# Block 0 of a fused layernorm, state-space and gated-MLP kernel: eps as the bias of the ScalarE root, and first gate matmuls in two halves of the contraction

## Chip, cores and metric

The kernel runs on one core of a Trainium2 chip. The metric is device time in microseconds of one execution of the whole program, smaller is better. Engines are named as in the profile: PE is TensorE, PEld its weight loads, DVE is VectorE, ACT is ScalarE, POOL is GpSimd, SP is the queue that issues most loads. A load "lands" when its data has arrived. A "hand-over" is the time from the end of one engine's instruction to the start of the instruction on another engine that waited for it. PSUM is the memory that TensorE writes its results to; the "contraction" is the sum over the 512 features, done in four chunks of 128.

## The reference

The input is one sequence of 2048 tokens of 512 features. Only the first part matters here: the layernorm feeds everything, and its first block of 512 tokens (four tiles of 128, "block 0") is what the machine waits for at the start.

```python
xn = (x - mean(x)) / sqrt(var(x) + 1e-5)          # x: [2048, 512], bf16
y_ssm = 2 * Re(scan(Lam_bar, xn @ B_bar.T) @ C.T) + xn * Dskip
y_mlp = (gelu(xn @ w_gate) * (xn @ w_up)) @ w_down  # w_gate, w_up: [512, 1376]
out = x + y_ssm + y_mlp
```

## The kernel before

The program lists operations with their reads and writes. A scheduler inside the kernel then orders them by a model of durations: TensorE and the SP queue keep the order in which the program lists them, while VectorE, ScalarE and GpSimd may be reordered.

The parts that the change touches, with cuts marked `# ...`:

```python
# loads: four x tiles on the SP queue, first gate weights on the ScalarE queue, then the rest on SP
for j in range(4):
    ld_x0(j)
ld_w(WG, WGc, ins["B_w_gate"], 0, "scalar").nb = 900.0     # gate columns 0..383
ld_w(WU, WUc, ins["B_w_up"], 0)                            # up columns 0..383
ld_w(WG, WGc, ins["B_w_gate"], 1)
ld_w(WU, WUc, ins["B_w_up"], 1)
# ...
def LN(b, js=range(4), on_act=False, after=()):
    # ...
    for j in js:
        V(bn_stats(X[tt]) -> ST[tt]);  V(bn_aggr(ST[tt]) -> MVt[b][j])      # abridged
    POOL(copy of the means)                                                  # abridged
    V(lambda e: e.tensor_scalar(sbq.ap, mv.ap[:, :, 1], EPS_BF16, None, ALU.add), D_TINY, [mv], [sbq], "sbq")
    if on_act:
        ACT(lambda e: e.activation(qb.ap, sbq.ap, ACTF.Sqrt), d_act(4), [sbq, SCR], [qb], "sqrt")
    else:
        POOL(...pow 0.5...)
    V(lambda e: e.reciprocal(rq.ap, qb.ap), 150, [qb], [rq], "rq")
    # ... VectorE: XN = (X - mean) * rq, tile by tile
# ...
def TR0(j, engs, first=None):        # TensorE transposes tile j; its copies out of PSUM go to engs
    per = KD // len(engs)            # "VA": VectorE copies contraction chunks 0,1; ScalarE chunks 2,3
    # ... for n, eng in enumerate(engs): transposes of half n, then the copy of half n
# ...
def GU_first(fts, early, banks):
    def mm(ft, u, j0, j1):           # u=0 gate, u=1 up; four matmuls over the contraction
        # ... for dk in range(KD): matmul(start=(dk == 0), stop=(dk == KD - 1)), reads XT0[j0:j1]
    for u in range(2):
        for ft in early:             # early = three groups of 128 columns
            mm(ft, u, 0, 1)          # 12 gate matmuls, then 12 up matmuls, on tile 0
    params()
    for ft in early:
        for u in range(2):
            mm(ft, u, 1, 2)          # then tile 1
    # ... then the first of the "late" groups (second weight chunks), transposes of tiles 2 and 3
# ...
PE(fwarm, ...)                       # 11 warm-up matmuls that do nothing useful
LN(0, [0, 1], True)                  # tiles 0 and 1: statistics, root on ScalarE
TR0(0, "VA")
TR0(1, "V", hbanks[0][4])
LN(0, [2, 3], True, [GATE["evT"]])   # tiles 2 and 3: a second root on ScalarE
```

Of the kernel before, what the change touches and what calls it, by code (L numbers as in the profile page):

```python
# [9 lines left out]
ALU = mybir.AluOpType  # L10
ACTF = mybir.ActivationFunctionType
# [335 lines left out]
NT, NB, KD, KP, KF = 16, 4, 4, 4, 11  # L347
# [4 lines left out]
EPS_BF16 = 1.0013580322265625e-05  # L352

def d_pe(n_list):
    return sum(n / 2.4 + 2.5 for n in n_list)
def d_dve_tt2x(n): return 100.0 + 0.52 * n
def d_dve_1x(n): return 100.0 + 1.04 * n
def d_dve_scan(n): return 90.0 + 2.08 * n
def d_dve_ts4x(n): return 220.0 + 0.26 * n
D_TINY = 160.0  # L360
def d_act(n, ptr=0): return 190.0 + 0.833 * n + 90.0 * ptr
# [3 lines left out]
def build(nc, ins, out):  # L365
    with ExitStack() as es:
# [6 lines left out]
        BANK = [Buf("bank%d" % i, "ps", i, i + 1) for i in range(8)]  # L373

        def ring(parent, name, n):
            return [A.sub(parent, "%s%d" % (name, i), i) for i in range(n)]
# [11 lines left out]
        XNT = ring(XNT_all, "XNT", NB)  # L388
# [22 lines left out]
        def cols(buf, b, j0, j1):  # L411
            per = (buf.hi - buf.lo) // (4 * NB)
            return Buf("%s_%d_%d" % (buf.name, b, j0), "sb", buf.lo + per * (4 * b + j0), buf.lo + per * (4 * b + j1),
                       buf.ap[:, b, j0:j1])
        XTk = [[Buf("XT%d_%d" % (b, i), "xt", 4 * b + i, 4 * b + i + 1) for i in range(4)] for b in range(NB)]
        XT0 = XTk[0]
        XTr = lambda b: XTk[b]
        WRM = A.alloc("WRM", [128], BF16)
        PROW = A.alloc("PROW", [128], BF16)
# [6 lines left out]
        EPS = A.alloc("EPS", [1], F32)  # L426
# [76 lines left out]
        wchunk = lambda ft: 0 if ft < 3 else (1 if ft < 7 else 2)  # L503

        V = lambda fn, dur, r, w, tag="", after=(): S.op("vector", fn, dur, r, w, tag, after)
        ACT = lambda fn, dur, r, w, tag="", after=(): S.op("scalar", fn, dur, r, w, tag, after)
        POOL = lambda fn, dur, r, w, tag="": S.op("gpsimd", fn, dur, r, w, tag)
        PE = lambda fn, dur, r, w, tag="": S.op("tensor", fn, dur, r, w, tag)
# [9 lines left out]
        SCR = A.alloc("SCR", [1], F32)  # L518
# [4 lines left out]
        def next_bank():  # L523
            b_ = rstate["n"] % 8
            rstate["n"] += 1
            return b_
# [69 lines left out]
        def LN(b, js=range(4), on_act=False, after=()):  # L596
            j0, j1 = js[0], js[-1] + 1
            mn, sbq, qb, rq = (cols(t, b, j0, j1) for t in (MN, SBQ, QB, RQ))
            mv = Buf("MV%d_%d" % (b, j0), "sb", MVt[b][j0].lo, MVt[b][j1 - 1].hi, MV[b].ap[:, j0:j1])
            for j in js:  # L600
                tt = 4 * b + j
                V(lambda e, tt=tt: e.bn_stats(ST[tt].ap, X[tt].ap), d_dve_1x(512), [X[tt]], [ST[tt]], "bnst", after)  # L602
                V(lambda e, tt=tt, j=j: e.bn_aggr(MVt[b][j].ap, ST[tt].ap), D_TINY, [ST[tt]], [MVt[b][j]], "bnag")  # L603
            POOL(lambda e: e.tensor_copy(mn.ap, mv.ap[:, :, 0]), 200, [mv], [mn], "mn")
            V(lambda e: e.tensor_scalar(sbq.ap, mv.ap[:, :, 1], EPS_BF16, None, ALU.add), D_TINY, [mv], [sbq], "sbq")  # L605
            if on_act:
                ACT(lambda e: e.activation(qb.ap, sbq.ap, ACTF.Sqrt), d_act(4), [sbq, SCR], [qb], "sqrt")  # L607
            else:
                POOL(lambda e: e.tensor_tensor(qb.ap, sbq.ap, HALF.ap[:, 0:j1 - j0], ALU.pow), 1100, [sbq, HALF], [qb], "pow")
            V(lambda e: e.reciprocal(rq.ap, qb.ap), 150, [qb], [rq], "rq")  # L610
            for j in js:
                tt = 4 * b + j
                xs = XN[tt % 8]
                V(lambda e, tt=tt, j=j, xs=xs: e.tensor_scalar(  # L614
                    xs.ap, X[tt].ap, mn.ap[:, j - j0:j - j0 + 1], rq.ap[:, j - j0:j - j0 + 1], ALU.subtract, ALU.mult),
                  d_dve_ts4x(512), [X[tt], mn, rq], [xs], "ln_n")
# [9 lines left out]
        def TR0(j, engs, first=None):  # L626
            if not TBANK:
                TBANK.extend([next_bank(), next_bank()])
            per = KD // len(engs)
            toks = [XT0[j]] if len(engs) == 1 else [Buf("XT0_%d_%d" % (j, n), "xt", j + n / len(engs), j + (n + 1) / len(engs))  # L630
                                                    for n in range(len(engs))]
            for n, eng in enumerate(engs):
                bank = TBANK[(j + n) % 2] if first is None else first
                pt = PS[bank].bitcast(BF16)

                def f(e, n=n, pt=pt):
                    ins_ = None
                    for q in range(per):
                        k = per * n + q
                        ins_ = e.transpose(pt[:, 128 * q:128 * (q + 1)], XN[j].ap[:, 128 * k:128 * (k + 1)], IDN.ap)  # L640
                    return ins_
                PE(f, 56.0 * per, [XN[j], IDN], [BANK[bank]], "T0")
                dst = XNT[0].ap[:, per * n:per * (n + 1), 128 * j:128 * (j + 1)]
                src = pt[:, 0:128 * per].rearrange("p (q t) -> p q t", q=per)
                if eng == "A":
                    GATE["evTA"] = ACT(lambda e, src=src, dst=dst: e.activation(dst, src, ACTF.Copy), d_act(128 * per),  # L646
                                       [BANK[bank]], [toks[n]], "evT")
                else:
                    GATE["evT"] = V(lambda e, src=src, dst=dst: e.tensor_copy(dst, src), 110 + 0.6 * 128 * per,
                                    [BANK[bank]], [toks[n]], "evT")  # L650
# [67 lines left out]

        def GU_first(fts, early, banks):

            def mm(ft, u, j0, j1):
                W, Wc = ((WG, WGc), (WU, WUc))[u]
                h, q0 = j0 // 2, 256 * u + 128 * (j0 % 2)
                bank = banks[h][ft]

                def f(e):
                    ins_ = None
                    for dk in range(KD):
                        ins_ = e.matmul(PS[bank][:, q0:q0 + 128 * (j1 - j0)], W.ap[:, dk, 128 * ft:128 * (ft + 1)],  # L729
                                        XNT[0].ap[:, dk, 128 * j0:128 * j1], start=(dk == 0), stop=(dk == KD - 1))  # L730
                    return ins_
                PE(f, d_pe([128 * (j1 - j0)] * 4), [Wc[wchunk(ft)]] + XT0[j0:j1], [BANK[bank]], "GU0")

            def evac(ft, h, after=()):
                bank, c0 = banks[h][ft], 256 * h
                GATE["nh"] = kk = (GATE["nh"] + 1) % 3
                GATE["last_gelu"] = ACT(lambda e: e.activation(GG[kk].ap[:, 0:256], PS[bank][:, 0:256], ACTF.Gelu_apprx_tanh),
                                        d_act(256), [BANK[bank]], [GG[kk]], "gelu", after)
                ACT(lambda e: e.activation(UPB[kk].ap[:, 0:256], PS[bank][:, 256:512], ACTF.Copy),
                    d_act(256), [BANK[bank]], [UPB[kk]], "evU")  # L740
                V(lambda e: e.tensor_tensor(HTt[0][ft].ap[:, c0:c0 + 256], GG[kk].ap[:, 0:256], UPB[kk].ap[:, 0:256], ALU.mult),
                  d_dve_tt2x(256), [GG[kk], UPB[kk]], [HTt[0][ft]], "hmul")

            for u in range(2):
                for ft in early:
                    mm(ft, u, 0, 1)
            params()
            for ft in early:
                for u in range(2):
                    mm(ft, u, 1, 2)  # L750
            late = [ft for ft in fts if ft not in early]
            mm(late[0], 0, 0, 2)
            TR0(2, "V")
            TR0(3, "A")
            for ft in early:
                evac(ft, 0, [GATE["evTA"]])
            for ft in late[1:]:
                mm(ft, 0, 0, 2)
            for ft in late:
                mm(ft, 1, 0, 2)  # L760
                evac(ft, 0)
            for ft in fts:
                for u in range(2):
                    mm(ft, u, 2, 4)
                evac(ft, 1)
# [130 lines left out]

        PE(fwarm, d_pe([512] * nwarm) * 1.6, [WRM], [BANK[wb]], "warm")
        LN(0, [0, 1], True)
        TR0(0, "VA")
        hbanks = [{ft: next_bank() for ft in range(5)} for h in range(2)]  # L900
        TR0(1, "V", hbanks[0][4])
        LN(0, [2, 3], True, [GATE["evT"]])
        load_B()
        GU_first(range(5), range(3), hbanks)
        tables_dve()
        GATE["before_gelu"] = [tables_act([GATE["last_gelu"]])]
# [82 lines left out]
```

## Time and profile before

| | before |
|---|---|
| median of the runs at first (three runs) | 179.61 us (179.39 to 179.63) |
| span of the profiled run | 177.6 us |
| TensorE busy | 173.4 us, 98% |
| first useful matmul (first gate matmul) starts | 6.62 us |
| last matmul starts | 175.09 us |

The profile page, first lines: the span, then busy time, share and instruction count of each engine.

```profile
span 177.6 us, 2527 instructions
PE 173.4 (98%) x927; PEld 86.5 (49%) x927; DVE 156.9 (88%) x277; ACT 91.0 (51%) x175; POOL 9.5 (5%) x20
```

The chain of waits of the kernel before, in order of time. Each line has the start in us, the length in us and what ran; "issue" is time in which nothing visible was waited for.

```profile
0.74 2.11 DMA arena<-in_A_x_dram
...
2.87 1.29 DVE arena L602 x2
4.16 0.23 DVE arena L603 x2
...
4.41 0.18 DVE arena L605
...
4.68 0.21 ACT arena L607
...
4.91 0.18 DVE arena L610
...
5.19 0.42 DVE arena L614
...
5.66 0.41 PE PS L640 x4
...
6.09 0.39 ACT arena L646
6.49 0.14 issue
6.62 1.50 PE PS L729 x24
...
142.42 32.91 PE PS L844 x171
```

L602 and L603 are the statistics, L605 the eps add, L607 the root, L610 the reciprocal, L614 the normalising, L640 the transposes, L646 the ScalarE copy and L729 the first gate and up matmuls. From 6.62 us on the chain is TensorE alone to the last matmul, so as long as TensorE's work stays the same, only an earlier start can shorten the kernel.

The timeline of the kernel before around the copies (start, length, engine, line, operation, shapes, count, and in brackets the idle time before it and what ended it):

```profile
5.66 0.72 PE L640 MATMUL PS<-arena 128*128 128x128 bf16 x8 [0.64 <-DVE arena L614]
5.98 0.86 DVE L649 COPY arena<-PS 128x256 bf16<-128x256 bf16 x2
6.09 0.38 ACT L646 ACTIVATE arena<-PS 128x256 bf16<-128x256 bf16 x1 [1.22 <-PE PS L640]
...
6.62 1.17 PE L729 MATMUL PS<-arena 128*128 128x128 bf16 x18 [0.24 <-ACT arena L646]
```

ScalarE has the half that is transposed second and takes 0.38 us; VectorE has the half that is transposed first (its first copy ends at 6.28 us in the trace). All first gate matmuls wait for both.

### The profile page before, as it was taken

The page shows a single profiled execution, that of the slowest core. Times are in us where ns is not written, and L with a number is a line of the kernel's source. Part 1 is how long each engine was busy: PE and PEld are TensorE (multiplying, and loading weights), DVE is VectorE, ACT ScalarE, POOL GpSimd, SP SyncE. Part 2 cuts the span into 40 slices and gives each one's busy share as a digit, 9 for nine tenths or more (in the row PEclk, how much of TensorE's full clock was granted, in tenths as well). Part 3 has the DMA queues.
Part 4 walks back from the last instruction along what each step waited for, and adds up shares of the span by engine and source line. Part 5 has one row for each costly group of instructions (what it writes and reads, how often), then busy time and mean ns, then how long its engine had stood idle before and what let it go on. Part 6 is the DMA issues. An engine that isn't in the chain of part 4 may idle for free.

```text
span 177.6 us, 2527 instructions
## 1 busy us (share of the span) xinstructions
PE 173.4 (98%) x927; PEld 86.5 (49%) x927; DVE 156.9 (88%) x277; ACT 91.0 (51%) x175; POOL 9.5 (5%) x20
## 2 busy tenths in 40 slices
PE   7899999999999999999999999999999999999994
PEld 2697464444644444444644444444464444444453
DVE  5859998998998999779999999899999999999411
ACT  3189999976486899002577495000658700620000
POOL 3020024000000002400000000000000000000000
PEclk9999999999999999999999999999999999999999
DMA  5999914989043000001024000000001000002211
GB/s 131 342 309 179 299 30 91 159 231 315 0 86 65 0 0 0 2 30 63 30 51 97 0 6 0 30 30 30 30 4 30 0 0 0 0 0 78 74 51 37
DMA packets 26387, 12.90 MB, mean 73 GB/s; under 512 B 17704, under 2 KB 26376, under 8 KB 26376
## 3 DMA queue, kind: packets, MB, share of 16 engines
q1 hardware_dynamic: 25824, 12.36, 27.3%
q10 hardware_dynamic: 552, 0.40, 0.9%
q8 instruction: 7, 0.11, 0.3%
q14 instruction: 4, 0.03, 0.1%
HBM read 6.46 MB, written 2.10 MB: 48 GB/s over the span
## 4 chain that ended last, share of the span: by engine, by line
PE 95%; DVE 1%; DMA 1%; ACT 0%; issue 0%; DVEq 0%; ACTq 0%
PE PS L844 37%; PE PS L804 34%; PE PS L667 16%; PE PS L729 5%; PE PS L778 3%; DMA arena<-in_A_x_dram 1%; DVE arena L602 1%; PE PS L640 0%; DVE arena L614 0%; ACT arena L646 0%; DVE arena L862 0%; DVE arena L603 0%; ACT arena L607 0%; DVE arena L605 0%; DVE arena L610 0%
## 5 line engine op out<-in xcount | busy, mean ns | idle before, releaser
L844 PE MATMUL PS<-arena 128*128 128x512 bf16 (+3 forms) x323 | 66.2, 366 | 0.0
L804 PE MATMUL PS<-arena 128*128 128x512 bf16 x280 | 61.7, 379 | 0.0
L844 PEld LDWEIGHTS PS<-arena 128*128 128x128 bf16 (+1 forms) x323 | 30.8, 98 | 35.2
L819 ACT ACTIVATE arena<-PS 128x512 bf16<-128x512 f32 x35 | 20.9, 599 | 46.9 <-PE PS L804 32.1
L804 PEld LDWEIGHTS PS<-arena 128*128 128x128 bf16 x280 | 27.3, 98 | 32.1
L700 DVE TENSOR_TENSOR_SCAN arena<-arena 128x512 bf16<-128x512 f32 x32 | 38.8, 1253 | 0.0
L667 PE MATMUL PS<-arena 128*128 128x512 bf16 x128 | 28.3, 379 | 0.0
L822 ACT ACTIVATE arena<-PS 128x512 bf16<-128x512 f32 x35 | 20.8, 597 | 4.7 <-PE PS L804 4.7
L667 PEld LDWEIGHTS PS<-arena 128*128 128x128 bf16 x128 | 12.5, 98 | 14.9
L862 DVE TENSOR_TENSOR arena<-PS,arena 128x512 bf16<-128x512 f32 (+2 forms) x17 | 10.9, 653 | 9.9 <-PE PS L844 9.9
L671 ACT ACTIVATE arena<-PS 128x512 bf16<-128x512 f32 x32 | 17.7, 596 | 3.4 <-PE PS L667 3.4
L824 DVE TENSOR_TENSOR arena<-arena 128x512 bf16<-128x512 bf16 x35 | 13.7, 417 | 2.7 <-ACT arena L822 2.6
L836 ACT ACTIVATE PS<-arena 128x512 f32<-128x512 bf16 (+2 forms) x17 | 9.6, 580 | 5.5 <-DVE arena L862 4.8
L602 DVE BATCH_NORM_STATS2 arena<-arena 128x6 f32<-128x512 bf16 x16 | 10.2, 684 | 1.4 <-DMA arena<-in_A_x_dram 1.2
L729 PE MATMUL PS<-arena 128*128 128x256 bf16 (+1 forms) x104 | 9.3, 248 | 0.2 <-ACT arena L646 0.2
L689 DVE TENSOR_TENSOR arena<-arena 128x4096 bf16<-128x4096 bf16 (+1 forms) x5 | 9.3, 1859 | 0.0
L687 DVE TENSOR_TENSOR arena<-arena 128x4096 bf16<-128x4096 bf16 (+1 forms) x5 | 9.3, 1858 | 0.0
L712 DVE TENSOR_TENSOR arena<-arena 128x4096 bf16<-128x4096 bf16 x4 | 9.1, 2284 | 0.0
L713 DVE TENSOR_TENSOR arena<-arena 128x4096 bf16<-128x4096 bf16 x4 | 9.1, 2283 | 0.0
L729 PEld LDWEIGHTS PS<-arena 128*128 128x128 bf16 x104 | 8.1, 98 | 1.0 <-issue 0.4
L621 DVE TENSOR_TENSOR arena<-arena 128x512 bf16<-128x512 bf16 x16 | 6.1, 416 | 0.0
L778 PE MATMUL PS<-arena 128*128 128x192 bf16 x64 | 5.9, 246 | 0.0
(84 smaller groups left out, 105.9 us busy)
## 6 DMA issues: line engine op xcount, KB each, us to landing
out_dram<-arena SPq DMA_DIRECT2D x15, 128.0 KB, 1.7
arena<-in_A_x_dram SPq DMA_DIRECT2D x3, 512.0 KB, 6.9
arena<-in_B_w_down_dram SPq DMA_DIRECT2D x1, 1280.0 KB, 6.6
arena<-in_A_x_dram SPq DMA_DIRECT2D x4, 128.0 KB, 3.0
arena<-in_B_w_gate_dram SPq DMA_DIRECT2D x1, 512.0 KB, 5.9
arena<-in_B_w_up_dram SPq DMA_DIRECT2D x1, 512.0 KB, 6.8
arena<-in_B_w_gate_dram SPq DMA_DIRECT2D x1, 480.0 KB, 4.1
arena<-in_B_w_up_dram SPq DMA_DIRECT2D x1, 480.0 KB, 5.2
```

Source lines behind the costliest of these rows:

```text
L602: V(lambda e, tt=tt: e.bn_stats(ST[tt].ap, X[tt].ap), d_dve_1x(512), [X[tt]], [ST[tt]], "bnst", after)
L667: ins_ = e.matmul(PS[bank][:, :], BBT[c][dk].ap[:, 128 * s:128 * (s + 1)], XNT[b].ap[:, dk, :], start=(dk == 0), stop=(dk == KD - 1))
L671: ACT(lambda e, bank=bank, k3=k3, s=s, c=c: e.activation(SSc[k3][s][c].ap, PS[bank][:, :], ACTF.Copy), d_act(512), [BANK[bank]], [SSc[k3][ ...
L700: V(lambda e, g=g, rb=rb, init=init: e.tensor_tensor_scan(g.ap, rb, g.ap, init, ALU.mult, ALU.add), d_dve_scan(512), [g, PA[RRr]] + ([CARc ...
L729: ins_ = e.matmul(PS[bank][:, q0:q0 + 128 * (j1 - j0)], W.ap[:, dk, 128 * ft:128 * (ft + 1)], XNT[0].ap[:, dk, 128 * j0:128 * j1], start=( ...
L778: ins_ = e.matmul(dst, XNT[b].ap[:, dk, 128 * j:128 * (j + 1)], WGU[:, :, dk, f0:f0 + m], start=(dk == 0), stop=(dk == KD - 1))
L804: ins_ = e.matmul(PS[bank][0:m, c0:c1], W.ap[:, dk, 128 * ft:128 * ft + m], XNT[b].ap[:, dk, c0:c1], start=(dk == 0), stop=(dk == KD - 1))
L819: GATE["last_gelu"] = ACT(lambda e, bg=bg, kk=kk, m=m: e.activation(GG[kk].ap[0:m, :], PS[bg][0:m, :], ACTF.Gelu_apprx_tanh), d_act(512), ...
L822: ACT(lambda e, bu=bu, kk=kk, m=m: e.activation(UPB[kk].ap[0:m, :], PS[bu][0:m, :], ACTF.Copy), d_act(512), [BANK[bu]], [UPB[kk]], "evU")
L824: V(lambda e, kk=kk, m=m, ft=ft, k2=k2: e.tensor_tensor(HTt[k2][ft].ap[0:m, :], GG[kk].ap[0:m, :], UPB[kk].ap[0:m, :], ALU.mult), d_dve_tt ...
L844: ins_ = e.matmul(PS[bank][:, c0:c1], l_[:, 128 * j:128 * (j + 1)], r_[:, c0:c1], start=False, stop=last and n == len(ops) - 1, skip_group ...
L862: V(lambda e: e.tensor_tensor(OUTB[ko].ap[:, c0:c1], PS[bank][:, c0:c1], XD[tt].ap[:, c0:c1], ALU.add), d_dve_1x(c1 - c0), [BANK[bank], XD ...
```

## The change

The intent is to start TensorE's useful work earlier. Step 1 removes the VectorE eps add in block 0 by giving eps to the ScalarE root as its bias. Step 2 swaps the engines that copy the two halves of tile 0 and splits the first twelve gate matmuls: the six that need the half with VectorE's copy run first, then the six of the other half.

```diff
+        XT0h = [Buf("XT0_0_%d" % n, "xt", n / 2, (n + 1) / 2) for n in range(2)]
 # ...
-            V(lambda e: e.tensor_scalar(sbq.ap, mv.ap[:, :, 1], EPS_BF16, None, ALU.add), D_TINY, [mv], [sbq], "sbq")
             if on_act:
-                ACT(lambda e: e.activation(qb.ap, sbq.ap, ACTF.Sqrt), d_act(4), [sbq, SCR], [qb], "sqrt")
+                ACT(lambda e: e.activation(qb.ap, mv.ap[:, :, 1], ACTF.Sqrt, bias=EPS.ap), d_act(4), [mv, EPS, SCR], [qb], "sqrt")
             else:
+                V(lambda e: e.tensor_scalar(sbq.ap, mv.ap[:, :, 1], EPS_BF16, None, ALU.add), D_TINY, [mv], [sbq], "sbq")
 # ...
-            def mm(ft, u, j0, j1):
+            def mm(ft, u, j0, j1, dks=range(KD), first=0, last=KD - 1, toks=None):
 # ... (its loop runs over dks, with start=(dk == first), stop=(dk == last); it reads toks or XT0[j0:j1])
-            for u in range(2):
+            for n in (1, 0):
                 for ft in early:
-                    mm(ft, u, 0, 1)
+                    mm(ft, 0, 0, 1, [2 * n, 2 * n + 1], 2, 1, [XT0h[n]])
+            for ft in early:
+                mm(ft, 1, 0, 1)
 # ...
-        TR0(0, "VA")
+        TR0(0, "AV")
```

More of the change, by code (lines that the diff above doesn't have):

```diff
@@ L629, in TR0 @@
             per = KD // len(engs)
-            toks = [XT0[j]] if len(engs) == 1 else [Buf("XT0_%d_%d" % (j, n), "xt", j + n / len(engs), j + (n + 1) / len(engs))
-                                                    for n in range(len(engs))]
+            toks = [XT0[j]] if len(engs) == 1 else XT0h
             for n, eng in enumerate(engs):
@@ L727, in f @@
                     ins_ = None
-                    for dk in range(KD):
+                    for dk in dks:
                         ins_ = e.matmul(PS[bank][:, q0:q0 + 128 * (j1 - j0)], W.ap[:, dk, 128 * ft:128 * (ft + 1)],
-                                        XNT[0].ap[:, dk, 128 * j0:128 * j1], start=(dk == 0), stop=(dk == KD - 1))
+                                        XNT[0].ap[:, dk, 128 * j0:128 * j1], start=(dk == first), stop=(dk == last))
                     return ins_
-                PE(f, d_pe([128 * (j1 - j0)] * 4), [Wc[wchunk(ft)]] + XT0[j0:j1], [BANK[bank]], "GU0")
+                PE(f, d_pe([128 * (j1 - j0)] * len(dks)), [Wc[wchunk(ft)]] + (toks or XT0[j0:j1]), [BANK[bank]], "GU0")
             def evac(ft, h, after=()):
```

## The prediction

> **What bounds the kernel.** TensorE. The page gives PE 173.4 us busy of a 177.6 us span; the chain of waits is 95% PE. In that chain PE runs without a break from 6.62 to 175.32 us, and successive matmul starts in the timeline show no late issue after 8.16 us. So only what comes before 6.62 us can pay. That stretch, in the timeline: x lands at 2.85, statistics to 4.37, eps add 4.41–4.58, root 4.68–4.88, reciprocal, normalise from 5.19, transposes 5.66–6.38, copies, first gate matmul 6.62 (PE idle 0.24 us before it, released by the ScalarE copy).
>
> **Step 1, eps as bias.** The add (0.17 us) and one hand-over leave the chain. A VectorE-to-ScalarE hand-over takes 0.10 us (4.58 to 4.68), so the root can start at about 4.47 instead of 4.68: −0.21 us. Against it, the bias becomes a pointer. The Trainium skill ("ScalarE: Activation LUTs", section "What ACT_TABLE_LOAD costs") gives about 93 ns for each [128,1] pointer operand; this trace has two 2048-wide sines, 2.011 us with such a bias and 1.946 us without, so 0.065 us. Today's root takes 0.203 us; I expect 0.27 to 0.30. Net about −0.12 us down to the transposes. The second root (8.69 us) is off PE's chain.
>
> **Step 2, halves.** Now all twelve first gate matmuls wait for both copies: VectorE's (5.98–6.28) and ScalarE's, which starts only after the second half's transposes (6.10) and takes 0.38 us, to 6.48; the matmul follows 0.14 us later. After the change ScalarE takes the half transposed first (to about 6.25) and VectorE the second (about 5.98 to 6.27), and the first six matmuls wait for VectorE's alone. With a hand-over of 0.10 to 0.14 us they start at about 6.39 instead of 6.62, step 1 included. ScalarE's half is there before the seventh (six take 0.33 us): no new wait. Step 2 alone is worth about 0.1.
>
> **What takes some back.** The up matmuls after the twelve gates would be due at 6.39 + 12 × 0.0555 = 7.06 us. Their weights land at 7.03 us in this trace, and the change doesn't move that transfer. So the earliness is capped there at about 0.2 us; if they land a little later, PE waits. Later loads have room: second gate chunk 9.01 (due about 9.3), second up chunk 10.44 (due 10.8), first B transpose 15.20 (due 16.05). All other matmul work stays equal.
>
> **Risk.** The kernel orders VectorE and ScalarE work by its own modelled schedule; a slightly changed start could reorder work over the whole kernel and open stalls, though PE's order is fixed.
>
> **Prediction.** 179.61 − 0.20 = 179.41 us. The runs of before already spread over 0.24 us, so the range is 179.10 to 179.75. Chances: faster by over 2% 0.005, within 2% 0.985, slower by over 2% 0.01.
>
> **What would show it.** Step 1: no VectorE add in the two first roots, a root of 0.27–0.30 us starting at about 4.47. Step 2: first gate matmul at about 6.39, released by the VectorE copy, PE idle before it under 0.2 us. Cap: first up matmul at about 7.1, perhaps waiting for its weights; PE unbroken after it, ending about 0.2 us earlier.
>
> **What would make it wrong.** The pointer bias costing as much as the add; up weights landing later than 7.1; a reordered VectorE or ScalarE stream that stalls PE later; a difference of 0.2 us lost in run-to-run spread.

## The result

| | before | after |
|---|---|---|
| median, first comparison (6 runs each) | 179.64 us (179.39 to 179.73) | 179.42 us (179.25 to 179.46) |
| ratio after / before | | 0.9988, 95% interval 0.9975 to 1.0001 |
| median, second comparison, another chip | 179.67 us (11 runs, 179.37 to 180.12) | 179.55 us (6 runs, 179.32 to 180.52) |
| ratio, second comparison | | 1.0002, 95% interval 0.9981 to 1.0024 |

A ratio compares the runs of the two kernels in the same rounds, and not their medians, so it is not quite the ratio of the medians quoted beside it. Both intervals hold 1. The first median fell on the predicted number almost exactly; the second comparison shows that this agreement alone proves little.

The profile page after:

```profile
span 177.6 us, 2525 instructions
PE 173.5 (98%) x927; PEld 86.4 (49%) x927; DVE 156.3 (88%) x275; ACT 91.5 (52%) x175; POOL 10.1 (6%) x20
```

Two instructions fewer, the two adds, and the same span. The chain of waits after (L603 and L604 are now the statistics, L607 the root, L611 the reciprocal, L615 the normalising, L649 the VectorE copy):

```profile
2.87 1.29 DVE arena L603 x2
4.16 0.23 DVE arena L604 x2
...
4.50 0.30 ACT arena L607
...
4.83 0.18 DVE arena L611
...
5.11 0.42 DVE arena L615
...
5.58 0.41 PE PS L640 x4
...
6.01 0.30 DVE arena L649
6.31 0.14 issue
6.45 0.83 PE PS L729 x12
7.28 0.03 issue
7.30 0.84 PE PS L729 x12
...
142.44 32.91 PE PS L846 x171
```

The first gate matmul comes at 6.45 us instead of 6.62 us. But the twelve gates are followed by a hole, the first up matmul starts at 7.30 us, and the last long piece starts at 142.44 us against 142.42 us before. The timeline of after and one line of its list of waits (who waited for what: us in total, times, longest) name the hole:

```profile
6.45 1.36 PE L729 MATMUL PS<-arena 128*128 128x128 bf16 x18
6.86 1.29 DVE L603 BATCH_NORM_STATS2 arena<-arena 128x6 f32<-128x512 bf16 x2
7.30 0.39 PEld L729 LDWEIGHTS PS<-arena 128*128 128x128 bf16 x7 [0.20 <-DMA arena<-in_B_w_up_dram]
```

```profile
PEld PS L729 <- DMA arena<-in_B_w_up_dram: 0.2, 1, 0.2
```

The weight load for the first up matmul waits 0.20 us for the up weights. In this run they landed at 7.26 us, in the profiled run of before at 7.03 us. So in this pair of traces the whole earliness was lost to one load. The times of these two runs say the same: 179.39 us before and 179.44 us after. The traced run of before is the fastest of its six; nothing shows what its slower runs (179.61 to 179.73 us) had lost.

### The profile page after: what moved, and what is told of

Its sections match the earlier page's. It is cut to its first block, busy times and chain, and to the rows that moved or that the text cites. A ratio compares the mean times of both kernels' runs of the same rounds, so it can differ in the third digit from the quotient of the medians.

```text
span 177.6 us, 2525 instructions
## 1 busy us (share of the span) xinstructions
PE 173.5 (98%) x927; PEld 86.4 (49%) x927; DVE 156.3 (88%) x275; ACT 91.5 (52%) x175; POOL 10.1 (6%) x20
## 4 chain that ended last, share of the span: by engine, by line
PE 95%; DVE 2%; DMA 1%; issue 0%; ACT 0%; ACTq 0%; DVEq 0%
PE PS L846 37%; PE PS L806 34%; PE PS L667 16%; PE PS L729 5%; PE PS L780 3%; DMA arena<-in_A_x_dram 1%; DVE arena L603 1%; PE PS L640 0%; DVE arena L615 0%; ACT arena L607 0%; DVE arena L649 0%; DVE arena L864 0%; DVE arena L604 0%; DVE arena L611 0%; PE PS L537 0%
## 5 line engine op out<-in xcount | busy, mean ns | idle before, releaser
L603 DVE BATCH_NORM_STATS2 arena<-arena 128x6 f32<-128x512 bf16 x16 | 10.1, 680 | 1.2 <-DMA arena<-in_A_x_dram 1.1
```

Source lines behind the costliest of these rows:

```text
L603: V(lambda e, tt=tt: e.bn_stats(ST[tt].ap, X[tt].ap), d_dve_1x(512), [X[tt]], [ST[tt]], "bnst", after)
```

## The experiments

Theory A: the change makes TensorE ready earlier, by an amount that the trace shows, and what is left at the end is decided by the first thing TensorE needs later: the up weights, then further loads. Rival B: the 0.22 us between the first medians is spread between runs. Rival C: the gain or loss comes from the reordered VectorE and ScalarE work later. More rivals are named with the runs. All twelve runs gave correct results, one of them (without eps) with a deliberate small error.

What every trace said, read from its records: landing of the first two x tiles, start of the first transpose, the distance from the second transpose to the third (about 56 ns at the full TensorE clock, about 107 ns at half), first gate matmul, landing of the first up weights, first up matmul, last matmul. All in us but the distance, in ns. The labels are those of the experiments.

| trace | x tiles land | first transpose | distance, ns | first gate | up weights land | first up | last matmul |
|---|---|---|---|---|---|---|---|
| before | 2.85, 3.42 | 5.66 | 55 | 6.623 | 7.03 | 7.290 | 175.09 |
| after | 2.85, 3.41 | 5.58 | 56 | 6.448 | 7.26 | 7.304 | 175.12 |
| c1_before_again | 2.84, 3.46 | 5.69 | 56 | 6.649 | 7.39 | 7.437 | 175.29 |
| c1_after_again | 2.78, 3.45 | 5.65 | 106 | 6.762 | 7.14 | 7.430 | 175.23 |
| c1_eps_only | 2.89, 3.38 | 5.61 | 56 | 6.574 | 7.32 | 7.364 | 175.18 |
| c1_halves_only | 2.88, 3.35 | 5.70 | 56 | 6.571 | 7.79 | 7.835 | 175.88 |
| c2_halves_ordered | 2.84, 4.22 | 6.44 | 56 | 7.316 | 8.10 | 8.144 | 175.96 |
| c2_before_up_early | 2.96, 3.33 | 5.77 | 106 | 6.941 | 7.33 | 7.608 | 175.41 |
| c2_after_up_early | 2.87, 3.37 | 5.66 | 107 | 6.761 | 7.16 | 7.467 | 175.27 |
| c2_swap_nosplit | 2.89, 3.44 | 5.66 | 107 | 6.766 | 7.53 | 7.574 | 175.39 |
| c3_split_noswap | 2.89, 3.46 | 5.66 | 106 | 6.552 | 7.09 | 7.218 | 175.27 |
| c3_noeps | 2.79, 3.36 | 5.65 | 107 | 6.761 | 7.10 | 7.428 | 175.23 |
| c3_before_gates_first | 2.84, 3.26 | 5.66 | 55 | 6.620 | 7.17 | 7.957 | 175.09 |
| c3_after_gates_first | 2.88, 3.42 | 5.61 | 56 | 6.476 | 6.94 | 7.813 | 174.94 |

Three things in this table vary from run to run whatever the kernel: when x lands, when the up weights land (6.94 to 8.10 us), and whether TensorE is at full clock by the transposes. One thing does not vary: in all fourteen, the time of the traced run is 4.29 to 4.34 us more than the start of its last matmul. So the time of a run, to about 0.05 us, tells when its TensorE work ended.

### The kernel before, unchanged (c1_before_again)

No edit.

> The kernel before, unchanged, against itself: a null control. Theory A (the change starts TensorE about 0.2 us earlier, and that earliness is real but capped by when the first up weights land): ratio 1.000 within 0.0005, and the first up matmul starts at the later of 7.28 us and 0.05 us after the up weights land. Rival B (the measured 0.22 us is run-to-run or chip-to-chip spread): medians of the same kernel on one chip differ by 0.1 to 0.25 us. In either case I want to see whether the landing of the up weights, 7.03 us in the first trace of before and 7.26 us in that of after, varies from run to run.

Median 179.55 us (179.37 to 180.16, 6 runs) against 179.67 us for the same kernel in the same rounds; ratio 1.0000, interval 0.9982 to 1.0018. The ratio is what theory A expects, and the spread is what rival B expects: two medians of one kernel on one chip differ by 0.12 us. In its trace the up weights land at 7.39 us and the first up matmul starts 0.046 us later, at 7.437. So before, too, pays for a late landing, and the landing varies by 0.36 us between two traces of one kernel.

### The changed kernel, unchanged (c1_after_again)

No edit.

> The changed kernel, unchanged, once more. Theory A: 0.1 to 0.2 us under before (ratio 0.9989 to 0.9995); first gate matmul again at 6.45 us (within 0.03), root of 0.296 us, first up matmul at the later of 7.12 us and 0.05 us after its weights land. Rival B: ratio within 0.0004 of 1.

Ratio 1.0002, interval 0.9981 to 1.0024: the expected 0.1 to 0.2 us were missed, and for the time rival B stands. The first gate matmul was at 6.762 us, not at 6.45: a miss that neither theory had foreseen. The root was in place (4.50 us, 0.295 us long) and the weights were not late. Its chain of waits shows what was:

```profile
0.99 4.88 PE PS L889 x11
5.86 0.44 PE PS L640 x4
6.30 0.02 issue
6.33 0.30 DVE arena L649
6.63 0.14 issue
6.76 1.50 PE PS L729 x24
```

The chain no longer goes through the layernorm: it runs through the eleven warm-up matmuls (L889). In this run TensorE's clock rose only at about 6.2 us. The normalised tile was ready at 5.52 us, but the warm-up matmuls, one each 0.427 us at half clock, still held TensorE; the first transpose started at 5.65 us, and the transposes went 107 ns apart instead of 56. In the first traces of before and after the clock rose at about 4.0 and 3.7 us. Six of the fourteen traces had half clock at the transposes; I call these late. The rise is spread, though, and does not come at two fixed times: it was at about 4.9 us in c1_halves_only and at about 5.4 us in c3_before_gates_first, both ahead of the transposes. (These times are from the spacing of the matmuls and from the granted clock that most traces record.) The Trainium skill ("TensorE: Matmul & The Clock Gate", section "What you observe") gives these two distances, 107 and 56 ns, and a transition "around 4µs into sustained matmul activity, ±500ns run-to-run". The distances agree. The time does not quite: counted from the first matmul at 0.99 us, the rise came 2.7 us later in the trace of after and over 5.4 us later in c3_noeps, where all eight transposes (the last at 6.40 us) still went at half clock.

### Step 1 alone (c1_eps_only)

```diff
-            V(... sbq = var + eps ...)
             if on_act:
-                ACT(... Sqrt of sbq ...)
+                ACT(... Sqrt of mv, bias=EPS.ap ...)
             else:
+                V(... sbq = var + eps ...)
```

> Step 1 alone. Theory A: root starts about 4.50 and takes 0.296 us; transposes at 5.58 instead of 5.66; first gate matmul at about 6.54 (0.085 us earlier than before), released by the ScalarE copy; time about 0.08 us under before, unless the up weights land after 7.15 us. Rival C (the gain comes from the reordered VectorE and ScalarE work later on and not from the start): time as in the full change whatever the start is, and late issues of TensorE after 8.2 us in before.

First gate matmul 6.574 us with x landing 0.04 us later than in the trace of before. Counted from the landing of the first x tile it is 3.687 us, against 3.778 us before: step 1 is worth 0.09 us. The up weights landed at 7.32 us and the first up matmul, due 0.667 us after the first gate at 7.24, waited until 7.364. Median 179.43 us (179.31 to 180.19), ratio 0.9998, interval 0.9977 to 1.0019. The mechanism is as theory A has it; the time tells nothing at this size. No late issue after 8.3 us was found in this trace or in that of before other than evenly spaced holes of one matmul, which are missing records; that speaks against rival C.

### Step 2 alone, as the scheduler orders it (c1_halves_only)

```diff
+            V(... sbq = var + eps ...)
             if on_act:
-                ACT(... Sqrt of mv, bias=EPS.ap ...)
+                ACT(... Sqrt of sbq ...)
```

(taken from the changed kernel; all else as after)

> Step 2 alone. Theory A: root 0.203 us at 4.68, transposes at 5.66 as before; first gate matmul at about 6.53 (0.09 us earlier than before), released by the VectorE copy; time about 0.09 us under before, unless the up weights land after 7.15 us.

First gate matmul 6.571 us, 3.692 us after the first x tile lands: step 2 is worth 0.09 us as well. From first transpose to first gate it is 0.873 us against 0.962 us before. But the median was 180.00 us (179.54 to 180.22), ratio 1.0017, interval 1.0000 to 1.0034. Two causes show in the trace. The first gate weights landed at 6.49 us, just in time, but the up weights at 7.79 us, so the first up matmul came 0.60 us later than it was due. And the scheduler had put a copy of an up result ahead of the second root on ScalarE:

```profile
9.38 0.38 ACT L739 ACTIVATE arena<-PS 128x256 bf16<-128x256 f32 x1 [2.98 <-PE PS L729]
9.66 0.20 ACT L608 ACTIVATE arena<-arena 128x2 bf16<-128x2 bf16 x1
...
9.89 0.17 DVE L611 RECIPROCAL arena<-arena 128x2 f32<-128x2 bf16 x1 [0.63 <-ACT arena L608]
10.16 0.73 DVE L615 TENSOR_SCALAR arena<-arena 128x512 bf16<-128x512 bf16 x2
10.63 0.55 PEld L640 LDWEIGHTS PS<-arena 128*128 128x128 bf16 x8 [0.24 <-DVE arena L615]
```

The copy (L739) had to wait for TensorE, the second root (L608) stood behind it, and tiles 2 and 3 were normalised about 1 us later than in the trace of after. TensorE's transposes of tile 2 came 0.125 us late for that and those of tile 3 another 0.089 us. This is the reordering that the prediction had listed as a risk. It did not strike in the change itself, where the second root goes first.

### Step 2 alone with the order kept by hand (c2_halves_ordered)

```diff
-                ACT(... Sqrt of sbq ...)
+                GATE["root"] = ACT(... Sqrt of sbq ...)
 # ... in the first tiles' copies:
-                ACT(... copy of the up result ..., "evU")
+                ACT(... copy of the up result ..., "evU", [GATE["root"]])
```

> Step 2 alone, with one order kept by hand: the first up copies of ScalarE may not go before its second root (in the first try of step 2 alone the kernel's own scheduler put one there, and the second pair of normalised tiles came 1 us later, a TensorE stall of 0.125 us at the third transpose). Theory A: second root near 8.7 us, no stall at the third tile's transposes; first gate matmul at 6.53 to 6.57 us; last matmul start = first up matmul + 167.80 us, as in the two first traces. Rival D (step 2 itself is harmful): up to 0.3 us over before again.

Median 179.58 us (179.40 to 180.25), ratio 0.9994, interval 0.9975 to 1.0014, on another chip than c1_halves_only. The stall at tile 2 is gone. So the ordering was a real cost of c1_halves_only in its trace; how much of its 0.0017 it makes cannot be said, since the two ran on different chips. The traced run was one of the slowest, 180.25 us, for another reason: the second x tile landed at 4.22 us instead of about 3.4 and the up weights at 8.10. The expected 6.53 to 6.57 was missed for that (7.316), but from first transpose to first gate it is again 0.874 us. Rival D, step 2 itself harmful, finds no support.

### The swap without the split (c2_swap_nosplit)

```diff
-            for n in (1, 0):
-                for ft in early:
-                    mm(ft, 0, 0, 1, [2 * n, 2 * n + 1], 2, 1, [XT0h[n]])
-            for ft in early:
-                mm(ft, 1, 0, 1)
+            for u in range(2):
+                for ft in early:
+                    mm(ft, u, 0, 1)
```

> The full change without its split of the gate matmuls: ScalarE still copies the first half and VectorE the second, but all twelve gate matmuls wait for both copies, as before. In the trace of the changed kernel the two copies end within 0.02 us of each other (6.28 and 6.30), so theory A2 says that swapping the engines does all of step 2 and the split nothing: first gate matmul at 6.45 us plus at most 0.03. Rival G (the split matters): 6.55 us or later.

The clock rose late, so the number to compare is the 6.762 us of c1_after_again, also late: 6.766 us. Once the engines are swapped the split adds nothing, because VectorE's half is the one that ends last anyway (6.62 against 6.50 us here; with an early clock, in the trace of after, 6.30 against 6.28).

### The split without the swap (c3_split_noswap)

```diff
-            for n in (1, 0):
+            for n in (0, 1):
                 for ft in early:
-                    mm(ft, 0, 0, 1, [2 * n, 2 * n + 1], 2, 1, [XT0h[n]])
+                    mm(ft, 0, 0, 1, [2 * n, 2 * n + 1], 0, 3, [XT0h[n]])
 # ...
-        TR0(0, "AV")
+        TR0(0, "VA")
```

> The full change with its split but without its swap: VectorE copies the first half as before, ScalarE the second, and the first six matmuls take VectorE's half. Theory A2 (swap or split alone does all of step 2): first gate matmul within 0.05 us of 6.45 with an early clock (of 6.76 with a late one); ScalarE's half, ready at about 6.40 us, is there before the seventh. Rival: a wait of over 0.05 us at the seventh matmul.

First gate matmul 6.552 us with a late clock, 0.21 us ahead of the two late traces above, and no wait at the seventh matmul (6.884 us, its half copied by 6.643). The expectation of equality was wrong. The reason is in the trace: the first half is transposed first, VectorE copies it from 6.115 to 6.406 us, and TensorE starts with it; in c1_after_again, whose first three transposes start within 0.01 us of the same times, VectorE gets the second half and starts only at 6.326. So the swap and the split work against each other: the change makes the twelve gates begin with the half that is ready last. The clock rose somewhat earlier here (between 5.98 and 6.06 us, against 6.2), which does not move that first half. With an early clock this version was not seen; an estimate from the trace of after is VectorE free at 5.85 us, copying to about 6.19, and a first gate at about 6.34 us instead of 6.45. The earliness was lost here too: TensorE waited 0.114 us for the second gate weights (landed 9.51 us) and 0.118 us for the second up weights (10.96 us), and the last matmul was at 175.27 us.

### The root without its bias (c3_noeps)

```diff
-                ACT(... Sqrt of mv, bias=EPS.ap ..., [mv, EPS, SCR], ...)
+                ACT(... Sqrt of mv ..., [mv, SCR], ...)
```

This leaves eps out of the first block.

> The full change without the eps in the two first roots (wrong by about 0.2% of the normalised values on purpose): no pointer operand. If the pointer is the whole of the longer root, the root takes 0.203 us again, starting at 4.50, and the transposes start at 5.49 us (0.09 us earlier), or later if the clock rises late and the warm-up matmuls still hold TensorE until about 5.65 us.

The root took 0.204 us instead of 0.295, so the pointer costs 0.09 us. The Trainium skill ("ScalarE: Activation LUTs", section "What ACT_TABLE_LOAD costs") says "each `[128,1]` pointer operand adds ≈ 93 ns"; 0.296 against 0.203 us in the traces of after and before is 0.093. Step 1 thus keeps about half of the roughly 0.18 us by which its root starts sooner. The clock rose late in this run, so the first transpose was held at 5.65 us and the first gate at 6.761 us, the same as in c1_after_again at 6.762, although the root began 0.09 us earlier. In this late-clock run the shorter root paid nothing.

### The load of the up weights moved ahead of the fourth x tile (c2_before_up_early, c2_after_up_early)

The same edit in both kernels:

```diff
-        for j in range(4):
+        for j in range(3):
             ld_x0(j)
         ld_w(WG, WGc, ins["B_w_gate"], 0, "scalar").nb = 900.0
         ld_w(WU, WUc, ins["B_w_up"], 0)
+        ld_x0(3)
```

> The kernel before with one load moved: the first up weights are fetched ahead of the fourth x tile. Theory A: they land near 6.4 us, about 0.8 us earlier, so they never decide; first up matmul = first gate matmul + 0.667 = about 7.29 us in every run; median 179.4 us and the spread over runs smaller than the 0.75 us of before in the last rounds, because late landings no longer show. Fourth x tile near 7.1 us, before VectorE asks for it at about 7.5. Rival E (what varies is the first x tile or the clock's rise, not the up weights): same median and spread as before.

> The changed kernel with the same load moved: the cap lifted. Theory A: first gate matmul 6.45 us, first up matmul at 6.45 + 0.667 = 7.12 us without a wait for weights; last matmul about 0.17 us earlier than in the traces of before and after (174.92 against 175.09 and 175.12), median about 179.2 us, 0.2 to 0.4 us under before in the same rounds. Rival F (another wait takes the earliness back after 7.1 us): a late issue elsewhere before 17 us.

Before with the edit: 179.61 us (179.36 to 179.82), ratio 0.9990, interval 0.9971 to 1.0009. After with the edit: 179.43 us (179.19 to 179.67), ratio to the kernel before 0.9980, interval 0.9963 to 0.9997. The slowest runs are gone in both (179.82 and 179.67 against 180.48 for before in these rounds), as theory A expects, with six runs each against eleven. The second interval is the only one of the ten in this document that lies below 1, and barely; it compares the change and the moved load together with the kernel before. But the expected medians, 179.4 and about 179.2 us, were missed, and so was the way there: the weights landed at 7.33 and 7.16 us, not near 6.4, while the fourth x tile slipped to 7.68 and 7.51 us. Both traces are late-clock ones, so the expected 7.12 us for the first up matmul could not be seen either (7.467 us, without a wait for weights). The medians favour theory A, but these traces do not prove it, and rival E of the expectation (what varies is x or the clock, not the up weights) stays open: in the trace of before with the edit x landed at 2.96 us, the latest of all, and the clock was late as well.

### The gates of tile 1 before the ups of tile 0 (c3_before_gates_first, c3_after_gates_first)

The same reordering in both kernels, no load moved. After:

```diff
             # twelve gate matmuls of tile 0, as in the change
+            for ft in early:
+                mm(ft, 0, 1, 2)          # gates of tile 1
             for ft in early:
                 mm(ft, 1, 0, 1)          # ups of tile 0
             params()
             for ft in early:
-                for u in range(2):
-                    mm(ft, u, 1, 2)
+                mm(ft, 1, 1, 2)          # ups of tile 1
```

> The changed kernel with TensorE's order altered and no load moved: the gate matmuls of the second tile go before the up matmuls of the first, so the first up weights are wanted 0.67 us later (6.45 + 24 x 0.0555 = 7.78 us). Theory A: no wait at the first up matmul unless its weights land after 7.74 us; then the first third-tile transpose is at about 9.78 us and the last matmul starts near 174.93 us where the clock rises early (before 5.5 us), near 175.2 us where it rises late. Second gate chunk is wanted at about 9.3 us, so a landing after that (9.0 to 9.5 seen) is the next cap. Time 0.2 to 0.35 us under before in the same rounds. Rival F (another wait takes the earliness back): a new late issue and a last matmul at 175.1 us or later with the clock early.

> The same order in the kernel before. Theory A: first gate matmul stays at 6.62 us (early clock), up weights wanted at 7.96 us, so they wait for nothing; last matmul at about 175.09 us as in the first trace of before; time 0.05 to 0.2 us under before, by the runs in which weights land late, and 0.1 to 0.2 us over the changed kernel in this order.

The two chains of waits, after with this order first, then before with it:

```profile
6.04 0.30 DVE arena L649
6.34 0.14 issue
6.48 2.17 PE PS L729 x36
...
142.27 32.91 PE PS L847 x171
```

```profile
0.99 4.69 PE PS L889 x11
5.68 0.39 PE PS L640 x4
...
6.09 0.39 ACT arena L646
6.49 0.14 issue
6.62 2.17 PE PS L729 x36
...
142.42 32.91 PE PS L846 x171
```

In both, 36 matmuls follow the first gate without a hole, and the last matmul starts at 174.94 and 175.09 us. The difference is 0.144 us (174.944 against 175.088), the same as that of the first gates (6.476 against 6.620). Here no load bit, and the earliness came through to the end undiminished; x had landed 0.04 us later in the first of the two. In the second the chain comes through the warm-up matmuls (L889), since the clock rose only at about 5.4 us; that cost nothing, as its first transpose came 2.816 us after x landed, just as in the trace of before. To be exact: in these two runs the up weights landed at 6.94 and 7.17 us, early enough for the old order too, so the pair shows that unhindered earliness is kept, not that this order saved it. That the order gives room until 7.8 us follows from the place of the first up matmul (7.813 us).

The times: 179.28 us (179.23 to 179.62, five runs), ratio to before 0.9991, interval 0.9979 to 1.0003; and 179.55 us (179.39 to 180.03), ratio 1.0007, interval 0.9994 to 1.0020. The first has the lowest median of all kernels here, 0.19 us under before, but its interval still holds 1, and the 0.2 to 0.35 us that had been expected were just missed. The second was expected 0.05 to 0.2 us under before and was not: its runs spread from 179.39 to 180.03 us, and at this size the medians are not resolved. The times of the two traced runs did follow: 179.28 and 179.39 us.

## Why the prediction was right, and where not

1. *TensorE bounds the kernel, and only what lies before 6.62 us can pay: right.* In all fourteen traces the last matmul starts 167.80 to 168.05 us after the thirteenth useful one. Eleven lie within 0.012 us of each other; the excess of the other three is accounted for, within 0.03 us, by waits for second weight chunks (c1_before_again 0.04, c3_split_noswap 0.23) or by the reordered root (c1_halves_only 0.21).
2. *Step 1, −0.12 us: the mechanism right, the size 0.09.* The root started at 4.496 us, not at 4.47, since the hand-over took 0.12 us and not the 0.10 of before; the root itself took 0.296 us, at the upper end of the range. The Trainium skill ("Perfetto Trace Analysis", section "Identifying Dependency Chains") says that instructions that wait on several engines may get EventSemaphore instructions ahead of them; in the trace one ran from 4.407 to 4.445 us ahead of this root. Before had one too, but of 0.017 us; this one took 0.038, and c3_noeps, whose root has no bias to wait for, had one of 0.017 us again and a hand-over of 0.10.
3. *Step 2, about 0.1 us: right in size* (0.09 us from first transpose to first gate). The predicted 6.39 us came out as 6.448, from the smaller step 1 and a hand-over of 0.145 us, just above the 0.10 to 0.14 that were allowed. What the prediction did not see is that the swap and the split overlap: the swap alone does it, and the split alone did more in its one, late-clock trace.
4. *"Their weights land at 7.03 us in this trace, and the change doesn't move that transfer. So the earliness is capped there at about 0.2 us": the cap right, its position wrong.* The landing is no constant: 6.94 to 8.10 us in fourteen traces. In six of the twelve that kept the order of the matmuls the first up matmul started 0.045 to 0.047 us after the landing, so the load decided; in the profiled run of after it took all of the gain. "Later loads have room" failed in the same way, in c1_before_again and c3_split_noswap.
5. *179.41 us: right, and partly by luck.* The sum, 0.20 us, is near what an undisturbed early-clock pair keeps (0.144 us in the pair of gates first, about 0.18 us when counted from the landing of x). The first comparison showed 0.22 us between medians, while its own profiled run had gained nothing (179.44 against 179.39 us), and the second comparison showed none. The prediction took 0.20 us off 179.61 us, a median of three runs, but read them from the trace of the fastest run, 179.39 us; that the slower runs of before lose about 0.2 us to something was not in its reckoning. A null control of the same size moves 0.12 us. So the medians do not resolve this change; both intervals lie within 0.25% of 1, well inside 2%. The fastest runs say a little more: of the 45 runs of before none is under 179.37 us, while the change had 2 of 12 under it (179.25 and 179.32), and the change with the load moved or the gates first 6 of 11 (down to 179.19). That is what an earliness of 0.1 to 0.2 us would look like that reaches the time only when nothing takes it back; it was seen afterwards and is not a test.
6. *The clock was missing from the prediction.* In the trace it was read from, the clock had risen at about 4 us. In six of fourteen traces it rose late. In five of these the warm-up matmuls held the first transpose to about 5.65 us; in the sixth, c2_before_up_early, x landed late and the first transpose came at 5.77. So in c1_after_again step 1 was worth next to nothing: 5.653 us against the 5.661 of before.

Open: how often the late clock occurs outside these fourteen runs, and what makes a landing late. Two of the slowest traced runs (180.17 and 180.25 us) had late landings; the slowest of all, 180.52 and 180.48 us, left no trace.

## What to carry to other kernels

When one engine is busy without a break from its first useful instruction to the end, only its start can move, and a start moved ahead is worth something only up to the next load that engine needs; so look up the slack of every load it meets afterwards, and do not take a landing time from one trace as a constant. Before splitting a dependency in two, ask which half is ready first and begin with that one. For effects of a tenth of a microsecond in 180, compare counted stretches inside traces of the same clock state, and run the unchanged kernel against itself to learn what the medians alone can tell.

## What the Trainium skill lacked or had wrong

- "TensorE: Matmul & The Clock Gate", section "What you observe": the rise is given as about 4 us into activity, ±500 ns. Here it came from 2.7 us (after) to 5.9 us (c2_after_up_early) after the first matmul of the kernel, so ±500 ns is too narrow. The distances of 107 and 56 ns agree.
- "TensorE: Matmul & The Clock Gate": I found nothing there on warm-up matmuls delaying useful work. Eleven of them, 512 columns wide and 0.427 us apart at half clock, held the first transpose until 5.65 us in a run in which the clock rose late.
- No page that I looked up tells how much the landing of one load varies from run to run: a 384 KB weight load in its place in the queue landed between 6.94 and 8.10 us, and the second 128 KB x tile between 3.26 and 4.22 us.
- "ScalarE: Activation LUTs", section "What ACT_TABLE_LOAD costs": the 93 ns for a pointer operand agree on a root of two columns (0.296 against 0.203 us), but not on the two sines of 2048 columns in the trace of before (2.011 us with a pointer bias, 1.946 without, so 65 ns). No run here tells why.
